# Norm factors of one batch spread by DMA, an FFN group moved, Newton steps one group sooner: attention, RMSnorm and FFN in one kernel

## The chip, the cores and the metric

One core of one Trainium2 chip. The metric is the device time of one execution in microseconds (us). The TensorE clock in the records was 0.998 to 1.0 of full speed, except where it is said otherwise.

## The reference

Eight batches of block-causal attention (8 heads, 576 positions, 64 dimensions a head) feed an RMS norm and a gated FFN (512 to 1536 and back) over all 4608 tokens.

```python
def _attn_ref(q, k, v):                       # q, k, v: 8 x 8 x 576 x 64
    scores = scale * np.matmul(q, k.transpose(0, 1, 3, 2))
    mask = block_i >= block_j                 # blocks of 64 positions
    scores = np.where(mask, scores, -1000000000.0)
    attn = np.exp(scores - max) ; attn = attn / sum     # shortened
    return np.matmul(attn, v)

def _moe_ref(x, w_gate, w_val, w_out, rms_g): # x: 4608 x 512
    rms = np.sqrt(np.mean(x * x, axis=-1, keepdims=True) + 1e-06)
    xn = x / rms * rms_g
    g = xn @ w_gate
    silu = g * (1.0 / (1.0 + np.exp(-g)))
    return silu * (xn @ w_val) @ w_out
```

## The kernel before

TensorE works through one stream in which the attention of one batch is interleaved with FFN work on the batch before. FFN work is dealt out in slots. A call of `group()` fills one slot: either an *up group* (8 matmuls of 512 columns, or 16 of 256 in the first twelve; then tanh on ScalarE and gs and HT on VectorE) or an *output group* (12 matmuls, evacuated by ScalarE alone). There are 108 up groups and 36 output groups in all. `later(k, fn)` runs `fn` k slots later. `mark(n)` says that the tokens below n lie scaled in XT, so that up groups may read them. PSUM is the memory into which matmuls write; its buffers come from two pools, and a matmul must wait until the buffer that it is to write has been read.

```python
    ps_s = ctx.enter_context(tc.tile_pool(name="ps_s", bufs=2, space=PSUM))   # scores, "sps"
    ps_f = ctx.enter_context(tc.tile_pool(name="ps_f", bufs=4, space=PSUM))   # all else, "fps"

    def group(n=1):
        for _ in range(n):
            ...
            if ready and have + 2 <= ui and far >= DOWN0 and (ui == len(ups) or 3 * di <= far - 3):
                ffn_down(*downs[di]); di += 1        # an output group when its turn has come
            elif up:
                ffn_up(*ups[ui]); ui += 1            # else an up group, if its tokens are in XT
            elif ready:
                ffn_down(*downs[di]); di += 1        # else an output group
            clear()
            gone += 1
            ...                                      # run what is due by now

    def ffn_up(n, m, k, lo, w):
        g = ps_f.tile([P, TOKC], FP32, name="fps")
        u = ps_f.tile([P, TOKC], FP32, name="fps")
        ...                                          # 4 matmuls into g, 4 into u
        nc.scalar.activation(out=th, in_=g, func=AF.Tanh, scale=0.5)
        nc.vector.scalar_tensor_tensor(out=gs, in0=th, scalar=1.0, in1=g, op0=ALU.add, op1=ALU.mult)
        nc.vector.tensor_mul(out=HT[n][...], in0=gs..., in1=u...)
```

The norm of a batch goes: sums and squares on TensorE, a transpose and ratios on VectorE, a root step (three small matmuls, then VectorE), two Newton steps of three operations each, and a last product S with a transpose to st. Then the 576 factors of each head must be spread over the partitions. `tail` does that with matmuls against a selection matrix (SELB), `late_tail` by way of DRAM with DMA.

```python
    def norm_spread(key):
        ...
        nc.vector.tensor_mul(out=s32[...], in0=rec[...], in1=y[...])                  # S
        nc.vector.transpose(st[:, 0:32 * n], s32[...])                                # st

    def norm_scale(key, b, j0, width, t):        # spread by matmul, scale from PSUM
        ...
        bc = ps_f.tile([P, 512], FP32, name="fps")
        if t < HP:
            nc.tensor.matmul(bc[:, 0:width], SELB[:, t, :], st[:, 0:width], start=True, stop=True)
            scale(t, j0, width, bc)
        else:
            ...                                  # four matmuls of 64 columns

    def norm_copies(b):                          # spread by DMA
        nc.sync.dma_start(out=rows, in_=nrm[b])                       # st to DRAM
        for a in range(2):
            nc.sync.dma_start(out=bc[a * D:(a + 1) * D], in_=rows....to_broadcast([D, HP, S]))

    def tail(b, k=6):
        norm_sums(b, b, WHOLE); norm_squares(b, b, WHOLE); norm_turn(b)
        if b > 1: norm_ratio(b, True)            # True: w2 summed and split into three bf16 terms
        else:     later(1, norm_ratio, b)
        later(2, norm_root, b)
        later(3, norm_newton, b, 0)
        later(3, norm_newton, b, 1)
        later(4, norm_spread, b)
        for u in range(HP + 1):
            later(k + u // 2, norm_scale, b, b, 0, 512, u)
        ...                                      # marks

    def late_tail(b):
        norm_sums(b, b, WHOLE); norm_squares(b, b, WHOLE); norm_turn(b); norm_ratio(b, True)
        later(2, norm_root, b)
        later(2, norm_newton, b, 0)
        later(3, norm_newton, b, 1)
        later(3, norm_spread, b)
        later(3, norm_copies, b)
        for t in range(HP):
            later(9 + t // 2, norm_apply, b, t)
        later(10, mark, b * S + S)

    for b, t in pairs:                           # batches 2..7, four pairs of heads each
        if (b, t) == (3, 0): ...; later(1, tail, 2, 4)
        e0 = scores_mm(b, t, 0); e1 = scores_mm(b, t, 1)
        scores_exp(*e0)
        group()
        scores_exp(*e1)
        if b > 3 or b == 3 and t == 0:
            group()
        ...
        e2 = scores_mm(b, t, 2)
        last = (b, t - 1) if t else (b - 1, HP - 1)
        outs = values_mm(*last, early=b == 2) if b > 3 or t else []   # early: fps, else sps
        scores_exp(*e2)
        ...
        group()
        evacuate(outs, b == 2)
        if t == 0:
            if b > 3: later(1, late_tail if b > 4 else tail, b - 1)
            scores_ends(b)
        if b > 3 or t == 0: group()
        ...
```

The softmax here doesn't subtract the row's maximum and nothing guards it: scores larger than these inputs give would overflow.

## Time and profile before

| | before |
|---|---|
| time, median of 4 runs | 399.22 us (399.04 to 399.74) |
| span of the profiled execution | 397.72 us |
| VectorE busy | 254.8 us |
| ScalarE busy | 197.3 us |
| moved by DMA | 39.38 MB |

A row of the timeline gives the start, the busy time, the engine, the line, the operation with its tiles and the number of instructions in the row. What stands in brackets is the idle time ahead of it and its releaser. Stalls are measured from start to start throughout, as the prediction explains; most changes between attention matmuls and the rest take 0.09 or 0.10 us more in these traces even where nothing waits, and are called changeovers here. Most rows are shown in the prediction. Two more, of batch 4's norm in the kernel before:

```profile
195.84 1.03 PE L496 MATMUL fps<-XT,WV 128*128 128x512 bf16 x4
196.95 2.75 PE L521 MATMUL fps<-WO,HT 128*128 128x512 bf16 x12
```

The starts are 1.11 apart where 0.866 is the plain pace of four: the stall of 0.25.

### The profile page before, as it was taken

The page shows a single profiled execution, that of the slowest core. Times are in us where ns is not written, and L with a number is a line of the kernel's source. Part 1 is how long each engine was busy: PE and PEld are TensorE (multiplying, and loading weights), DVE is VectorE, ACT ScalarE, POOL GpSimd, SP SyncE. Part 2 cuts the span into 40 slices and gives each one's busy share as a digit, 9 for nine tenths or more (in the row PEclk, how much of TensorE's full clock was granted, in tenths as well). Part 3 has the DMA queues.
Part 4 walks back from the last instruction along what each step waited for, and adds up shares of the span by engine and source line. Part 5 has one row for each costly group of instructions (what it writes and reads, how often), then busy time and mean ns, then how long its engine had stood idle before and what let it go on. Part 6 is the DMA issues. An engine that isn't in the chain of part 4 may idle for free.

```text
span 397.7 us, 7820 instructions
## 1 busy us (share of the span) xinstructions
PE 381.0 (96%) x3064; PEld 180.8 (45%) x3064; DVE 254.8 (64%) x640; ACT 197.3 (50%) x285; POOL 128.3 (32%) x181
## 2 busy tenths in 40 slices
PE   8889899999989999999999999999999899999996
PEld 3457665444434444344444444444344344444443
DVE  4788676567967578657716786478638967654430
ACT  3825871466548655455546564566453233332321
POOL 8927764846039204207446700100020010100000
PEclk9999999999999999999999999999999999999999
DMA  8999999999949919609999995200230020100112
GB/s 110 167 202 190 193 145 153 160 152 163 149 49 135 151 29 92 82 0 120 187 148 153 136 117 114 81 2 1 78 104 2 15 86 28 26 29 26 50 38 98
DMA packets 142677, 39.38 MB, mean 99 GB/s; under 512 B 129457, under 2 KB 139953, under 8 KB 142641
## 3 DMA queue, kind: packets, MB, share of 16 engines
q0 software_dynamic: 108448, 26.75, 69.3%
q1 hardware_dynamic: 33504, 12.00, 19.3%
q8 instruction: 24, 0.39, 0.4%
q10 hardware_dynamic: 688, 0.13, 0.2%
q14 instruction: 13, 0.10, 0.1%
HBM read 41.16 MB, written 10.03 MB: 129 GB/s over the span
## 4 chain that ended last, share of the span: by engine, by line
PE 76%; DVE 11%; DMA 5%; POOL 3%; ACT 2%; issue 1%; DVEq 0%; POOLq 0%
PE fps L496 39%; PE fps L521 23%; PE sps L244 5%; PE sps L293 4%; DMA WG<-in_moe_w_gate_dram 3%; DVE HT L504 3%; DVE gs L502 2%; PE fps L333 2%; DMA nt<-in_q_dram 2%; PE fps L293 1%; POOL VB L126 1%; POOL nt L112 1%; DVE st L426 1%; ACT PT L253 1%; ACT th L500 1%
## 5 line engine op out<-in xcount | busy, mean ns | idle before, releaser
L496 PE MATMUL fps<-XT,WG 128*128 128x512 bf16 (+1 forms) x480 | 112.1, 359 | 3.9 <-DVE gs L502 1.9
L502 DVE SCALAR_TENSOR_TENSOR gs<-th,fps 128x512 bf16<-128x512 f32 x108 | 73.9, 684 | 58.4 <-ACT th L500 58.2
L496 PE MATMUL fps<-XT,WV 128*128 128x512 bf16 (+1 forms) x480 | 111.0, 358 | 0.0
L253 ACT ACTIVATE PT<-sps 128x1024 bf16<-128x1024 f32 (+1 forms) x96 | 93.2, 988 | 30.7 <-PE sps L244 30.3
L500 ACT ACTIVATE th<-fps 128x512 f32<-128x512 f32 x108 | 64.6, 598 | 77.1 <-PE fps L496 74.1
L521 PE MATMUL fps<-WO,HT 128*128 128x512 bf16 (+1 forms) x444 | 97.1, 373 | 0.1
L504 DVE TENSOR_TENSOR HT<-gs,fps 128x512 bf16<-128x512 bf16 x108 | 74.3, 688 | 12.3 <-PE fps L496 0.9
L496 PEld LDWEIGHTS <-WV 128*128 128x128 bf16 x480 | 46.9, 98 | 47.1 <-issue 1.0
L496 PEld LDWEIGHTS <-WG 128*128 128x128 bf16 x480 | 42.4, 97 | 52.4 <-issue 17.2
L521 PEld LDWEIGHTS <-HT 128*128 128x128 bf16 x444 | 42.6, 98 | 50.5 <-issue 3.0
L525 POOL DMA_DIRECT2D out_dram<-osb x22 | 12.6, 571 | 153.2 <-ACT osb L523 151.3
L523 ACT ACTIVATE osb<-fps 128x512 f32<-128x512 f32 (+1 forms) x37 | 21.7, 586 | 78.7 <-PE fps L521 68.6
L126 POOL DMA_DIRECT2D VB<-in_v_dram x48 | 39.5, 847 | 6.0 <-DMA nt<-in_q_dram 2.7
L244 PE MATMUL sps<-QT,KT 64*128 64x192 bf16 (+5 forms) x280 | 32.3, 308 | 3.1 <-DVE KT L209 1.0
L119 POOL DMA_DIRECT2D nt<-in_q_dram x30 | 26.3, 876 | 7.0 <-DMA VB<-in_v_dram 4.0
L119 POOL DMA_DIRECT2D nt<-in_k_dram x30 | 26.3, 877 | 6.5 <-DMA VB<-in_v_dram 2.9
L319 DVE TENSOR_TENSOR SQ<-OT 128x512 bf16<-128x512 bf16 (+1 forms) x44 | 15.9, 372 | 10.2 <-ACT OT L317 9.3
L293 PEld LDWEIGHTS <-VB 128*64 128x64 bf16 x344 | 14.5, 109 | 13.1 <-issue 5.2
L441 DVE SCALAR_TENSOR_TENSOR XT<-OT,gscale,fps 128x64 bf16<-128x64 bf16 (+5 forms) x36 | 15.0, 477 | 8.0 <-PE fps L448 8.0
L244 PEld LDWEIGHTS <-KT 64*128 64x128 bf16 x280 | 8.8, 94 | 24.8 <-issue 19.6
L529 POOL DMA_DIRECT2D out_dram<-osb x12 | 6.5, 544 | 41.3 <-ACT osb L523 41.3
L226 DVE MEMSET PT<- 64x64 uint32 x95 | 8.9, 112 | 14.3 <-ACT PT L253 11.1
(77 smaller groups left out, 227.7 us busy)
## 6 DMA issues: line engine op xcount, KB each, us to landing
out_dram<-osb POOLq DMA_DIRECT2D x22, 256.0 KB, 2.4
VB<-in_v_dram POOLq DMA_DIRECT2D x32, 128.0 KB, 6.1
nt<-in_q_dram POOLq DMA_DIRECT2D x24, 128.0 KB, 6.7
nt<-in_k_dram POOLq DMA_DIRECT2D x24, 128.0 KB, 7.3
bc<-rows SPq DMA_DIRECT2D x8, 288.0 KB, 4.7
WG<-in_moe_w_gate_dram POOLq DMA_DIRECT2D x4, 384.0 KB, 9.6
WV<-in_moe_w_val_dram POOLq DMA_DIRECT2D x4, 384.0 KB, 10.8
WO<-in_moe_w_out_dram POOLq DMA_DIRECT2D x4, 384.0 KB, 7.8
```

The source lines that it names most:

```text
L119: nc.gpsimd.dma_start(out=nt[0:rows, 0:512].rearrange("p (h d) -> p h d", h=H), in_=src[b, :, c * P:c * P + rows, :].rearrange("h p d -> p ...
L126: nc.gpsimd.dma_start(out=vb[r:r + n, cc, :].rearrange("p (h d) -> p h d", h=H), in_=v[b, :, tok:tok + n, :].rearrange("h p d -> p h d"))
L244: nc.tensor.matmul(sp[:, a, o:o + w], KT[b][r, t, c * P:(c + 1) * P], QT[b][r, t, q0:q0 + w], start=True, stop=True, skip_group_check=True)
L253: nc.scalar.activation(out=pt[:, :, lo:lo + width], in_=sp[:, :, 0:width], func=AF.Exp, scale=SCALE)
L293: nc.tensor.matmul(ov[a * D:(a + 1) * D, o:o + w], vb[:, c, h * D:(h + 1) * D], rhs, start=(i == 0), stop=(i == len(chunks) - 1), skip_gro ...
L319: nc.vector.tensor_mul(out=sq, in0=o, in1=o)
L496: nc.tensor.matmul(acc[:, i * w:(i + 1) * w], wt[c][:, p, r * P:(r + 1) * P], XT[:, p, x0:x0 + w], start=(p == 0), stop=(p == HP - 1), ski ...
L500: nc.scalar.activation(out=th, in_=g, func=AF.Tanh, scale=0.5)
L502: nc.vector.scalar_tensor_tensor(out=gs, in0=th, scalar=1.0, in1=g, op0=ALU.add, op1=ALU.mult)
L504: nc.vector.tensor_mul(out=HT[n][:, m:m + k, lo:lo + w], in0=gs.rearrange("p (k w) -> p k w", k=k), in1=u.rearrange("p (k w) -> p k w", k=k))
L521: nc.tensor.matmul(po[:, 0:step], HT[n][:, m, i * P:(i + 1) * P], WO[:, m, o:o + step], start=(m == 0), stop=(m == NMC - 1))
L523: nc.scalar.mul(out=osb[:, o:o + step], in_=po[:, 0:step], mul=0.5)
```

## The change

The intent: let the norm factors of batch 3 go by DMA as those of later batches already do, take the Newton steps of batches 1 and 2 a slot sooner so that TensorE waits less for st, and put one FFN group fewer ahead of the last score step of batch 4's first pair.

```diff
@@ tail
         later(2, norm_root, b)
-        later(3, norm_newton, b, 0)
-        later(3, norm_newton, b, 1)
-        later(4, norm_spread, b)
+        later(2, norm_newton, b, 0)
+        later(2, norm_newton, b, 1)
+        later(3, norm_spread, b)
@@ loop over the pairs
-        if b > 3 or b == 3 and t == 0:
+        if b > 3 and (b, t) != (4, 0) or (b, t) == (3, 0):
             group()
@@
-                later(1, late_tail if b > 4 else tail, b - 1)
+                later(1, late_tail, b - 1)
```

## The prediction

> **What bounds the kernel now.** I read the page first (busy shares and the chain that ended last), then the timeline around the norm of batch 2, of batch 3, and of the later batches whose norm factors already go by DMA.
>
> ```profile
> span 397.7 us, 7820 instructions
> ...
> PE 381.0 (96%) x3064; PEld 180.8 (45%) x3064; DVE 254.8 (64%) x640; ACT 197.3 (50%) x285; POOL 128.3 (32%) x181
> ...
> PE 76%; DVE 11%; DMA 5%; POOL 3%; ACT 2%; issue 1%; DVEq 0%; POOLq 0%
> ```
>
> TensorE is busy 381.0 of 397.7 us at full clock, so what can be won is matmuls taken away, or gaps in its stream closed. A busy share cannot show a short gap, because overlapping matmul records hide it; I therefore take starts. In the chain of waits twelve output matmuls of 512 columns take 2.59 us, 0.216 each; a row of four takes 0.866. A start that comes later than that is a stall. Counted so, the stalls over 0.1 us after the first 60 us make about 9 us. One of the largest is ahead of the scaling of batch 2:
>
> ```profile
> 110.71 0.17 DVE L403 TENSOR_SCALAR y<-sh 128x18 int32<-128x18 int32 x1
> ...
> 110.73 2.76 PE L521 MATMUL fps<-WO,HT 128*128 128x512 bf16 x12
> 110.80 0.68 DVE L502 SCALAR_TENSOR_TENSOR gs<-th,fps 128x512 bf16<-128x512 f32 x1
> 111.58 0.69 DVE L504 TENSOR_TENSOR HT<-gs,fps 128x512 bf16<-128x512 bf16 x1
> 112.18 0.17 DVE L410 SCALAR_TENSOR_TENSOR z<-y 128x18 f32<-128x18 f32 x1
> ...
> 113.45 0.20 DVE L423 TENSOR_TENSOR S<-rec,y 128x36 bf16<-128x36 f32 x1
> ...
> 113.69 0.78 DVE L426 STREAM_TRANSPOSE st<-S 128x576 bf16<-128x576 bf16 x1
> ...
> 114.52 0.59 PE L448 MATMUL fps<-st,SELB 128*128 128x512 bf16 x2 [1.02 <-DVE st L426]
> ```
>
> The output group started at 110.73 and should have made room at 113.32; the spreading matmuls start at 114.52, 1.2 us late, released by st. This is the wait that the Newton part aims at. What the reader is to see is that VectorE has no hole between 110.71 and 114.47: gs, HT, six Newton steps at 0.21 us each, S, st, one behind the other.
>
> Batch 3 pays for its spread on TensorE and once more behind it:
>
> ```profile
> 156.89 0.59 PE L448 MATMUL fps<-st,SELB 128*128 128x512 bf16 x2
> ...
> 157.41 0.39 PE L244 MATMUL sps<-QT,KT 64*128 64x320 bf16 x4
> ...
> 161.11 0.59 PE L448 MATMUL fps<-st,SELB 128*128 128x512 bf16 x2
> ...
> 161.55 0.59 PE L496 MATMUL fps<-XT,WG 128*128 128x512 bf16 x2
> ...
> 162.33 0.38 PE L496 MATMUL fps<-XT,WG 128*128 128x512 bf16 x1 [0.19 <-DVE XT L441]
> ...
> 162.99 0.38 PE L496 MATMUL fps<-XT,WG 128*128 128x512 bf16 x1 [0.28 <-DVE XT L441]
> ...
> 164.07 0.28 PE L452 MATMUL fps<-st,SELB 128*128 128x64 bf16 x4
> ...
> 164.28 0.58 PE L244 MATMUL sps<-QT,KT 64*128 64x512 bf16 x4
> ```
>
> The spreading matmuls hold the stream for 0.52 + 0.44 + 0.21 = 1.17 us (start to the next start). The first FFN group on the new tokens then waits twice for XT: 162.33 instead of 161.98, and 162.99 instead of 162.55, 0.79 us in all.
>
> The later batches show what a DMA spread costs instead:
>
> ```profile
> 237.59 1.03 PE L496 MATMUL fps<-XT,WV 128*128 128x512 bf16 x4
> 239.01 1.02 PE L496 MATMUL fps<-XT,WG 128*128 128x512 bf16 x4 [0.40 <-DVE gs L502]
> ```
>
> For batch 5 the stream should go on at 238.45 and does so at 239.01, 0.56 us late: Newton, S, st and a square sit ahead of gs on VectorE, and gs gives back the PSUM buffer that the next group needs. By the same subtraction batch 6 loses 0.92 (at 280.56), batch 4 only 0.25 (at 196.95); batch 4 has an output group, which needs VectorE for nothing, among its FFN groups there.
>
> **What the Trainium skill says.** "Perfetto Trace Analysis", Identifying the Most-Contended Engine: matmul busy time is no good measure of headroom, since pipelined records mislead. The trace agrees: 96% busy, and a stall of 1.2 us is listed as 1.02. "TensorE: Matmul & The Clock Gate", Back-to-back issue gap: about 216 ns for 512 columns for isolated matmuls, but about 131 ns sustained in a stream with weight loads. This trace has weight loads ahead of all of them and shows 216; I use that. "VectorE: DVE Perf Modes", The DRAIN you can't avoid: an operation does not start until the one before has drained, so operation count is what to save. The Newton steps, 18 elements each, stand 0.21 us apart here: moving them saves none. "DMA: Bandwidth & Descriptors", Two DMAs through the same engine are not ordered: a DMA that reads what another wrote must wait for its completion. Here bc is issued 4.6 us after rows for batch 4 (196.03 to 200.66) and 1.8 us for batch 6.
>
> **The change part by part.**
>
> Newton sooner. This touches batches 1 and 2 only. In batch 1 the instruction order of VectorE comes out the same. In batch 2 the six Newton steps now precede gs and HT of the last FFN group before the output group; spread comes before the output group's slot instead of after. But output groups put nothing on VectorE, so the same instructions stand ahead of st as before, with no hole among them, and st still ends at about 114.5. The six steps (6 x 0.21 = 1.3 us) now delay gs and HT: HT ends at about 113.55 instead of 112.27, and the twelfth output matmul, which reads it and was due at 113.11, waits some 0.45 us. That comes out of the 1.2 us that TensorE waits anyway. Gain 0.0; perhaps 0.1 lost through the score exponential behind the later output evacuation.
>
> Batch 3 by DMA. Eight matmuls go with their loads: -1.17 us. The scaling on VectorE becomes four operations of 0.81 us from SBUF, issued while output groups run, nine and ten group slots after the sums: the waits for XT go, -0.79 us. New: rows and two bc transfers on SyncE, and a possible wait of gs behind st as in the other batches. An output group comes directly after the root step, so Newton, S and st fall in its 2.6 us: I take 0.05 us.
>
> One group less ahead of batch 4's last score step. The group is moved, not removed: 108 up and 36 output groups stay. What changes is the time that ScalarE has for the exponentials. With a single group there, batch 3 shows this wait:
>
> ```profile
> 128.00 0.39 PE L244 MATMUL sps<-QT,KT 64*128 64x320 bf16 x4
> ...
> 128.70 0.22 PE L293 MATMUL sps<-P,VB 128*64 128x64 bf16 x2 [0.30 <-ACT PT L253]
> ```
>
> The scores take 0.33 us, so the value matmuls are 0.37 late. For batch 4: the second exponential ran 133.54 to 134.45 before; the scores would now start at 133.71 and the values be due at 134.04, so about 0.4 us is new.
>
> Everything later comes one group sooner. In batch 4's norm no output group falls among the FFN groups any more (the last four of that stretch come in a row earlier). It then looks like batches 5 and 6: (0.56 + 0.92) / 2 = 0.74 instead of 0.25, +0.49 us.
>
> Sum: -1.17 - 0.79 + 0.05 + 0.40 + 0.49 + 0.0 to 0.1, about -1.0 us. **399.26 - 1.0 = 398.3 us.**
>
> **The rivals.** First, the Newton step removes the 1.2 us: then 397.1. For it: the releaser named is st, and Newton is in its chain. Against: the VectorE queue without a hole. It would need gs or HT to stand behind st instead of ahead. Second, bc is late for batch 3. For batch 4 VectorE waited for it, and the group that reads XT comes soon after:
>
> ```profile
> 208.56 1.55 DVE L477 SCALAR_TENSOR_TENSOR XT<-OT,gscale,bc 128x576 bf16<-128x576 bf16 x2 [3.50 <-DMA bc<-rows]
> ...
> 212.92 1.04 PE L496 MATMUL fps<-XT,WG 128*128 128x512 bf16 x4
> ```
>
> The last scaling ended at 212.54, 0.4 us ahead. Batch 3 has the same four output groups and value matmuls ahead of its reader, and around 140 to 157 the DMA engines have less to do (65 GB/s against 162 in 180 to 197); two microseconds later than there would cost one or two: 399.5 to 400.5. Third, the shifted groups clump VectorE work elsewhere: worth 0.5 us each way at most, by the stalls that batches 5 to 7 show. Fourth, the move is free (no wait on the exponential, batch 4's stall unchanged): then -1.9, 397.4.
>
> **Range and chances.** The removed 1.96 us are the surest part; the three additions (0.9 together) may lie between 0.2 and 1.7. Runs before spread over 0.7 us. So 397.3 to 399.4. Two per cent are 8 us, more than all the stalls concerned together: faster 0.01, within 0.985, slower 0.005.
>
> **What would show it.** Right: the matmul count falls by 8; st of batch 2 still ends 3.7 to 3.9 us after y of the root step, and the wait ahead of its spreading matmuls plus one inside the output group before it still sums to about 1.2; no wait for XT at the first group of batch 3's tokens; value matmuls in batch 4's first pair waiting 0.3 to 0.5 on ScalarE; a wait on gs of over 0.4 us in batch 4's norm. Wrong: st of batch 2 a microsecond earlier; bc of batch 3 landing after the output groups; a new wait over 0.5 us on a transpose or on K or Q.

## The result and the profile after

| | before | after |
|---|---|---|
| median | 399.22 us (4 runs) | 398.01 us (397.46 to 398.09, 4 runs) |
| span of the profiled execution | 397.72 | 396.24 |
| VectorE busy | 254.8 | 254.6 |
| ScalarE busy | 197.3 | 197.3 |
| moved by DMA | 39.38 MB | 40.11 MB |

The ratio is 0.9965 (95% interval 0.9947 to 0.9982). A ratio is the mean time of one kernel's fast runs over that of the other's of the same rounds, so it is not quite the ratio of the medians quoted. 398.3 had been predicted, with a range of 397.3 to 399.4. All outputs are right.

The page of the kernel after, in its first lines and the shares of the chain that ended last:

```profile
span 396.2 us, 7766 instructions
...
PE 376.6 (95%) x3016; PEld 180.1 (45%) x3056; DVE 254.6 (64%) x636; ACT 197.3 (50%) x285; POOL 128.4 (32%) x181
...
PE 77%; DVE 9%; DMA 5%; POOL 4%; ACT 3%; issue 2%; DVEq 0%; POOLq 0%
```

The weight loads tell the true count: 3056 instead of 3064, eight fewer. The matmul records are 48 fewer, because 40 of them are missing from this trace. So the fall of PE's busy time from 381.0 to 376.6 is no measure of the gain. The VectorE share of the chain fell from 11% to 9%.

The timeline of the kernel after, around batch 2's norm:

```profile
113.62 0.39 PE L521 MATMUL fps<-WO,HT 128*128 128x512 bf16 x1 [0.33 <-DVE HT L504]
113.71 0.78 DVE L426 STREAM_TRANSPOSE st<-S 128x576 bf16<-128x576 bf16 x1
114.54 0.59 PE L448 MATMUL fps<-st,SELB 128*128 128x512 bf16 x2 [0.53 <-DVE st L426]
```

st starts at 113.71 where it started at 113.69, and the spreading matmuls at 114.54 where they started at 114.52. The single wait of 1.20 us has become two: 0.49 ahead of the last output matmul, which now waits for a later HT, and 0.70 ahead of the spread, 1.19 together.

Batch 3's scaling on VectorE, in the kernel after:

```profile
161.21 1.55 DVE L477 SCALAR_TENSOR_TENSOR XT<-OT,gscale,bc 128x576 bf16<-128x576 bf16 x2 [0.87 <-DMA bc<-rows]
...
166.26 1.55 DVE L477 SCALAR_TENSOR_TENSOR XT<-OT,gscale,bc 128x576 bf16<-128x576 bf16 x2
```

and the first group that reads those tokens, on TensorE:

```profile
168.19 1.04 PE L496 MATMUL fps<-XT,WG 128*128 128x512 bf16 x4
```

VectorE waited 0.87 us for bc, with nothing else to do. The last scaling ended at 166.26 + 1.55 = 167.81, 0.4 us ahead of its reader, as batch 4's did before. There is no wait for XT any more.

Batch 4's first pair, and batch 4's norm sixty microseconds later, both in the kernel after:

```profile
133.95 0.39 PE L244 MATMUL sps<-QT,KT 64*128 64x320 bf16 x4
...
134.65 0.22 PE L293 MATMUL sps<-P,VB 128*64 128x64 bf16 x2 [0.30 <-ACT PT L253]
```

```profile
192.86 1.03 PE L496 MATMUL fps<-XT,WV 128*128 128x512 bf16 x4
194.29 1.02 PE L496 MATMUL fps<-XT,WG 128*128 128x512 bf16 x4 [0.41 <-DVE gs L502]
```

The values start 0.70 after the scores instead of 0.33 (135.53 to 135.86 in the kernel before): 0.37 lost there. Measured as a stall it is 0.46, but 0.09 of that is the changeover, which the kernel before has too. In the norm the next group starts 1.43 after the last instead of 0.866: a stall of 0.57, where it was 0.25.

The two traces, stage by stage, against the terms of the prediction (us; the sizes are starts against starts):

| term | predicted | measured |
|---|---|---|
| batch 3's spread and its waits for XT | -1.17 - 0.79 + 0.05 = -1.91 | -1.77 |
| Newton sooner, batch 2 | 0.0 to +0.1 | +0.14 |
| value matmuls wait for an exponential | +0.40 | +0.38 |
| batch 4's wait for gs | +0.49 | +0.32 |
| batch 6's wait for gs, 0.92 to 0.57 | not foreseen | -0.35 |
| last matmul to the end of the span, 4.09 to 3.89 | not foreseen | -0.20 |
| sum | about -1.0 | -1.48 (span: -1.48; medians: -1.21) |

For the first row: from batch 3's sums to batch 4's sums it took 42.41 us before and 41.50 after. The stretch after holds one up group less (8 x 0.216 = 1.73) and one output group more (2.59), so 0.86 us more work: -0.91 - 0.86 = -1.77. No wait for gs is seen in batch 3's norm. The third row is from the start of batch 4's first scores to batch 3's sums (9.36 us before, 8.01 after with one up group less, 1.73).

### The profile page after: what moved, and what is told of

Its sections match the earlier page's. It is cut to its first block, busy times and chain, and to the rows that moved or that the text cites. A ratio compares the mean times of both kernels' runs of the same rounds, so it can differ in the third digit from the quotient of the medians.

```text
span 396.2 us, 7766 instructions
## 1 busy us (share of the span) xinstructions
PE 376.6 (95%) x3016; PEld 180.1 (45%) x3056; DVE 254.6 (64%) x636; ACT 197.3 (50%) x285; POOL 128.4 (32%) x181
## 2 busy tenths in 40 slices
DMA packets 143364, 40.11 MB, mean 101 GB/s; under 512 B 129504, under 2 KB 140640, under 8 KB 143328
## 4 chain that ended last, share of the span: by engine, by line
PE 77%; DVE 9%; DMA 5%; POOL 4%; ACT 3%; issue 2%; DVEq 0%; POOLq 0%
PE fps L496 40%; PE fps L521 23%; PE sps L244 5%; PE sps L293 4%; DMA WG<-in_moe_w_gate_dram 3%; DVE HT L504 2%; PE fps L333 2%; DMA nt<-in_q_dram 2%; DVE gs L502 2%; PE fps L293 1%; ACT PT L253 1%; POOL VB L126 1%; POOL nt L112 1%; DVE st L426 1%; ACT th L500 1%
## 5 line engine op out<-in xcount | busy, mean ns | idle before, releaser
L496 PE MATMUL fps<-XT,WG 128*128 128x512 bf16 (+1 forms) x460 | 110.3, 358 | 4.7 <-DVE gs L502 1.9
L477 DVE SCALAR_TENSOR_TENSOR XT<-OT,gscale,bc 128x576 bf16<-128x576 bf16 (+2 forms) x24 | 15.9, 714 | 1.1 <-DMA bc<-rows 0.9
```

The costliest lines, as they stand in the source:

```text
L496: nc.tensor.matmul(acc[:, i * w:(i + 1) * w], wt[c][:, p, r * P:(r + 1) * P], XT[:, p, x0:x0 + w], start=(p == 0), stop=(p == HP - 1), ski ...
```

## The experiments

Eight kernels on one chip shared the runs of the kernel before: 399.40 us (399.32 to 399.77, 9 runs). The last two ran later on another chip.

### Newton steps alone

The kernel before with the first hunk of the change only.

```diff
-        later(3, norm_newton, b, 0)
-        later(3, norm_newton, b, 1)
-        later(4, norm_spread, b)
+        later(2, norm_newton, b, 0)
+        later(2, norm_newton, b, 1)
+        later(3, norm_spread, b)
```

> The kernel before with the Newton part alone (Newton two group slots and spread three slots after the sums of the first norms). My theory: VectorE's queue has no hole between the root step and st of batch 2, so st ends at the same time (y of the root step to the start of st: 2.98 us, as before), the 1.2 us wait only splits in two (about 0.5 inside the output group, 0.7 ahead of the spreading matmuls), and the time changes by 0.0 to +0.15 us. Rival: the wait was for Newton, st comes about 1 us sooner and the time falls by 1.0 to 1.2 us.

Measured: 399.41 us (399.20 to 400.04), ratio 1.0 (0.9987 to 1.0014). TensorE in its timeline:

```profile
113.50 0.39 PE L521 MATMUL fps<-WO,HT 128*128 128x512 bf16 x1 [0.33 <-DVE HT L504]
...
114.42 0.59 PE L448 MATMUL fps<-st,SELB 128*128 128x512 bf16 x2 [0.53 <-DVE st L426]
```

The same two waits, 0.49 and 0.70, with nothing else changed. The rival that sooner Newton steps remove the 1.2 us is out.

### DMA for batch 3 alone

The kernel before with the third hunk only.

```diff
-                later(1, late_tail if b > 4 else tail, b - 1)
+                later(1, late_tail, b - 1)
```

> The kernel before with only batch 3's factors spread by DMA; the group ahead of batch 4's scores stays. My theory: -1.17 us for eight matmuls and -0.79 for the waits for XT; +0.25 for a wait on gs in batch 3's norm (an output group stands ahead of its root step, as in batch 4 before); +0.32 because batch 4's norm loses its output group already by this part (0.57 instead of 0.25). Sum -1.4 us, which would be more than the whole change gave in the traces when their noise is taken off (-1.0). Rival, as the prediction put it: the wait in batch 4's norm comes from dropping the group, then -1.7 here and 0.25 us kept in batch 4's norm.

Measured: 397.68 us (397.05 to 398.03), ratio 0.9954 (0.9941 to 0.9966): -1.7 where -1.4 had been expected. TensorE in batch 4's norm:

```profile
195.13 1.03 PE L496 MATMUL fps<-XT,WV 128*128 128x512 bf16 x4
...
196.55 1.02 PE L496 MATMUL fps<-XT,WG 128*128 128x512 bf16 x4 [0.40 <-DVE gs L502]
```

1.42 between the starts: the wait for gs is 0.56 here already, without the moved group. Batch 3's own norm has a wait of 0.25 at 154.50. Batch 6's wait is 0.56 instead of 0.92, which is about the 0.35 us by which this run was better than expected. By its time alone the run would fit the rival as well, which said -1.7 with the 0.25 of batch 4 kept; the 0.56 in the trace is what rules that out.

### The moved group alone

The kernel before with the second hunk only.

```diff
-        if b > 3 or b == 3 and t == 0:
+        if b > 3 and (b, t) != (4, 0) or (b, t) == (3, 0):
```

> The kernel before with only the group ahead of batch 4's last score step dropped. My theory: +0.46 us by the value matmuls of batch 4's first pair that wait for the exponential; the waits for XT at batch 3's first group stay (0.79 us); batch 4's wait on gs goes from 0.25 to under 0.1, since an output group then follows its root step. Sum +0.2 us, between 0.0 and +0.5. Rival (the prediction's): batch 4's wait grows to 0.57, then +0.8 us.

Measured: 399.32 us (398.97 to 399.56), ratio 0.9995 (0.9982 to 1.0007). TensorE in batch 4's first pair:

```profile
134.09 0.22 PE L293 MATMUL sps<-P,VB 128*64 128x64 bf16 x2 [0.31 <-ACT PT L253]
```

and in batch 4's norm:

```profile
194.07 1.03 PE L496 MATMUL fps<-XT,WV 128*128 128x512 bf16 x4
194.94 1.03 PE L496 MATMUL fps<-XT,WG 128*128 128x512 bf16 x4
```

The wait of the values is there, 0.47 with the changeover. Batch 4's wait for gs is not: 0.87 between the starts is the plain pace, so even the 0.25 of before is gone. So the group's move costs 0.38, gives 0.25 back, and leaves +0.13. The trace shows +0.14, when the 0.44 us by which this execution was already ahead at 30 us are taken out. The medians show -0.08 where +0.2 had been expected: the spread of the runs does not resolve so little, and the sign rests on the trace alone. The kernel after, however, has 0.57 in batch 4's norm. With the run before, this puts that wait to the DMA part. The way there is read from the code and the traces: the tokens of batch 3 are marked ready later, output groups bridge the time in a row (five with the DMA part alone, from 154.50 on, four in the kernel after, two in the kernel before), and none is left to fall among batch 4's norm.

### The change without its Newton part

The kernel after with the first hunk undone; it serves as the base of the next experiments.

> The changed kernel with the Newton steps and the spread of the first norms put back to three and four slots. My theory: it is as fast as the changed kernel or 0.15 us faster; the wait ahead of batch 2's spreading matmuls is 1.2 us in one piece again, and the step of 0.14 us that the changed kernel loses at the value matmuls after it goes away. Rival: 1.0 to 1.2 us slower than the changed kernel.

Measured: 397.81 us (397.31 to 398.85; the slowest at a clock of 0.996), ratio 0.996 (0.9947 to 0.9972). The wait of 1.19 ahead of the spread is in one piece again. Span 396.13 against 396.24: the Newton part gains nothing, and costs 0.1 us if anything.

### Fewer VectorE operations ahead of st

The last kernel, with batch 2's ratio not split into three bf16 terms: six small operations fewer in the VectorE queue, and two fp32 terms instead of three bf16 ones in the matmuls of the root step.

```diff
-        if b > 1:
-            norm_ratio(b, True)
+        if b == 2:
+            norm_ratio(b)
         else:
             later(1, norm_ratio, b)
```

> The changed kernel with the old Newton places, and batch 2's norm ratio without its split in three bf16 terms: six small VectorE operations (6 x 0.21 = 1.28 us) fewer ahead of st, two fp32 terms in the root step instead. If the wait ahead of batch 2's spreading matmuls is set by the length of a VectorE queue without holes, st ends some 1.2 us sooner against the root step's neighbours and the 1.2 us wait goes to under 0.1; fp32 matmuls in the root step cost some 0.3 to 0.4 (0.52 busy for four in batch 1's root step against 0.22 for three bf16). Net against the kernel with the old Newton places: -0.7 to -0.9 us. If st waits for something else than its queue, it does not move and the time rises by 0.3.

Measured: 397.06 us (396.77 to 397.24), ratio 0.9937 (0.9923 to 0.995), so -0.75 against the base and -0.66 in the span. VectorE in its timeline:

```profile
112.73 0.78 DVE L426 STREAM_TRANSPOSE st<-S 128x576 bf16<-128x576 bf16 x1
```

and TensorE:

```profile
113.56 0.59 PE L448 MATMUL fps<-st,SELB 128*128 128x512 bf16 x2 [0.32 <-DVE st L426]
...
114.73 0.22 PE L293 MATMUL sps<-P,VB 128*64 128x64 bf16 x2 [0.25 <-ACT PT L253]
```

st starts at 112.73, 1.0 us earlier than the 113.74 of the base. The wait for it is 0.49 instead of 1.19, because the output group ahead of it comes earlier too (110.48 instead of 110.79: a wait of 0.49 for HT at 108.42 in the base is gone as well). Of the 1.0 us not all arrives: the scores now come closer behind the exponential, and the values behind them wait 0.41 on ScalarE. The expectation that under 0.1 of the wait would be left was a miss for that reason; the net was met. The place of the Newton steps is worth nothing and the number of operations is worth nearly a microsecond: what is ahead of st in the queue is the cause.

### The other Newton order in the later batches

The kernel after, with the second Newton step of `late_tail` a slot sooner, ahead of a gs and an HT.

```diff
         later(2, norm_newton, b, 0)
-        later(3, norm_newton, b, 1)
+        later(2, norm_newton, b, 1)
```

> The changed kernel with the second Newton step of the later batches (3 to 7) in the group of the root step, so 0.64 us less VectorE work stands between that group's gs and the next one's. A reader of the waits alone would expect the wait on gs in batches 4 to 6 (0.57 each) to vanish, -1.7 us or more. My theory: VectorE has no hole from the root step to that gs either, the work ahead of it is the same, and the wait stays at 0.57: 0.0 us, within 0.2.

Measured: 397.66 us (397.27 to 398.17), ratio 0.9955 (0.9942 to 0.9967), span 396.38. TensorE in batch 5's norm:

```profile
235.62 1.02 PE L496 MATMUL fps<-XT,WG 128*128 128x512 bf16 x4 [0.40 <-DVE gs L502]
```

The waits of batches 4, 5 and 6 are 0.57, 0.56 and 0.56, as in the kernel after (0.57 each). Batch 7's 0.88 came out as 0.32 + 0.57. The same rule, shown in other places: an instruction moved within a queue without a hole changes nothing for what stands behind both places.

### An output group behind the root step

The change without its Newton part, with an output group put by force right behind the root step of batches 4 to 7.

```diff
-            if ready and have + 2 <= ui and far >= DOWN0 and (...):
+            if ready and gone in (56, 72, 88, 102) or ready and have + 2 <= ui and far >= DOWN0 and (...):
```

> The changed kernel with the old Newton places, and one output group (no VectorE work) put directly after the root step of batches 4 to 7 in place of later. If the wait on gs in these norms comes from VectorE falling behind in an unbroken row of FFN groups, it goes: -0.57 for each of batches 4, 5, 6 and -0.88 for the one behind batch 7's st; the 1.0 us around batch 7's root step stays. Sum -2.6 us against the kernel with the old Newton places, so about 395.2 us. If the prediction's cause (the group count ahead of the scores) is what matters, nothing changes.

Measured: 396.29 us (396.23 to 396.58), ratio 0.9921 (0.9908 to 0.9935). All waits for gs in the four norms are gone, 2.58 us. But only 1.5 us of them arrive: 395.2 had been expected, a miss. TensorE at the first group on batch 7's tokens:

```profile
320.64 0.38 PE L496 MATMUL fps<-XT,WG 128*128 128x512 bf16 x1 [0.35 <-DVE XT L477]
321.37 0.38 PE L496 MATMUL fps<-XT,WG 128*128 128x512 bf16 x1 [0.35 <-DVE XT L477]
```

With the output group spent earlier, this group follows directly behind the scaling of its tokens and waits twice, 0.51 + 0.52 = 1.03. That the waits vanish as foretold fits their cause: too much VectorE work per TensorE work in that stretch. An output group, which brings VectorE nothing, lets it catch up. What TensorE waits for there is a PSUM buffer that gs gives back; whether more buffers would do as well was not tried.

### Batch 3's values in another PSUM pool

The change without its Newton part, with the value matmuls of batch 3 written to the pool of four banks (fps) instead of that of the scores (sps).

```diff
-        outs = values_mm(*last, early=b == 2) if b > 3 or t else []
+        apart = b < 4 or (b, t) == (4, 0)
+        outs = values_mm(*last, early=apart) if b > 3 or t else []
+        if (b, t) == (4, 0):
+            outs.append(head_product(3, ps_f.tile([P, 512], FP32, name="fps")))
```

> The changed kernel with the old Newton places, and the values of batch 3 accumulated in a bank of the other PSUM pool, so that they don't wait for the second exponential to free its bank. If that bank is what the value matmuls wait for, the waits of 0.35, 0.47 and 0.47 us at batch 3's pairs and batch 4's first go (-1.3 us) and possibly the 0.58 and 0.15 ahead of the scores behind them (up to -2.3); the dropped group then costs nothing. If they wait for the exponential's own data, nothing goes.

Measured: 395.94 us (395.71 to 396.36), ratio 0.9912 (0.9899 to 0.9926). ScalarE and TensorE in batch 4's first pair:

```profile
131.92 0.91 ACT L253 ACTIVATE PT<-sps 128x896 bf16<-128x896 f32 x1
132.18 0.39 PE L244 MATMUL sps<-QT,KT 64*128 64x320 bf16 x4
132.50 0.22 PE L293 MATMUL fps<-P,VB 128*64 128x64 bf16 x2
```

0.32 between scores and values where the kernel after has 0.70; the exponential still runs, until 132.83, when the values start. All the waits of this kind in batch 3 (0.35, 0.47, 0.47) and those ahead of the score matmuls there (0.58, and some of 0.10 to 0.15) are down to the changeover, and the time is 1.9 us below that of the base. The spans differ by 1.94, of which 0.34 had already come by 101 us, ahead of the edit's first effect, so some 1.6 us are the edit's by the traces. So the term "+0.40" of the prediction is not a wait for the result of an exponential. The value matmuls, which are those of the pair before, do not need it: they wait until ScalarE has read the bank (the PSUM buffer) that they are to write.

### The change again, and all that helped together

On another chip, the change unchanged, and a kernel with the last three edits (operations, output group, pool), no Newton part, and batch 7's tokens marked ready a slot later, against the wait that the output group had brought.

```diff
-        later(10, mark, b * S + S)
+        later(11 if b == B - 1 else 10, mark, b * S + S)
```

> The changed kernel once more, unchanged, in five rounds, so that it can be set beside the single parts, which had five rounds each. By the sum of the traces it should lie 0.2 to 0.4 us above the kernel with only the DMA part (397.68) and 0.1 to 0.2 above the one without the Newton part (397.81): 397.9 to 398.1. If the parts were worth what the change's order suggests, it would be the fastest of the three.

> All that the runs found to pay, together: DMA spread for batch 3, the dropped group, old Newton places, the values of batch 3 in the other PSUM pool (-1.9 by its run), an output group after each root step (-2.6), the ready mark of batch 7 one slot later so that the group reading XT does not come right behind its scaling (the new wait of 1.0 us in the run with the output groups), and batch 2's ratio without its split (-0.75). If these waits are independent, 397.81 - 1.9 - 2.6 - 0.75 = 392.6 us, all waits on gs in the norms gone; if they hide behind one another, between that and 394.5.

Measured, the change again: 397.73 us (397.26 to 398.14, 6 runs), below the 397.9 to 398.1 expected. Against 397.68 of the DMA part alone and 397.81 without the Newton part, the three can't be told apart by time; only the spans of the traces (396.24 and 396.34 for the change, 395.90 and 396.13 for the others) put them in the order that was expected. The kernel before had 401.01 us here (398.83 to 401.76, 11 runs), six of its runs at a clock of 0.991 to 0.996, so the recorded ratios of this call to it (0.9929 for the change; 0.9797, 0.9769 to 0.9825, for all together, verdict "unclear") are not leaned on.

All together: 392.36 us (391.95 to 392.78, 5 runs), 0.9865 of the change on the same chip, where 392.6 had been expected. Against the five runs of the kernel before at full clock (398.83 to 399.81 on this chip) it is some 1.7% faster by the means (392.4 over 399.3), an estimate from few runs. Its busy times:

```profile
PE 378.4 (97%) x3057; PEld 179.9 (46%) x3057; DVE 255.7 (65%) x630; ACT 196.9 (50%) x285; POOL 128.6 (33%) x181
```

No wait for gs in a norm is left; what is left are single stalls of 0.3 to 0.7 us.

## Why the prediction was right, point by point

**Newton sooner: right.** The wait split into 0.49 + 0.70, where 0.45 of the 1.2 had been predicted for the first; the part alone took 399.41 against 399.40. The loss of "perhaps 0.1" was 0.14 in the trace, at the place named: the values at 115.51 start 0.44 after their scores instead of 0.32. The reason given, a queue without a hole, is shown from two sides: the order of the Newton steps changes nothing in batch 2 nor in batches 4 to 7, and six operations fewer bring st 1.0 us forward.

**Batch 3 by DMA: right.** -1.77 instead of -1.91. The term -1.17 was mis-sized: counted to the next start it holds 0.10 of changeover twice, which the stream has without these matmuls too. The matmuls themselves take 4 x 0.216 + 4 x 0.029 = 0.98, and -0.98 - 0.79 is the measured -1.77. The term taken as +0.05, a wait for gs of its own, is nothing in the kernel after, and 0.25 in the DMA part alone. The last scaling was in time by the predicted 0.4 us, so the second rival is out.

**The moved group: right in size, its cause left open.** 0.38 instead of 0.40. The prediction reckoned with the end of the second exponential and did not say why the values have to wait for it. The other pool shows that it is not for the result: the values wait for ScalarE to free the scores' bank.

**Batch 4's wait for gs: right in direction by luck, with a wrong cause.** +0.32 was measured; +0.49 was predicted, because the mean of batches 5 and 6 (0.74) was taken where 0.57 came out. That mean held batch 6's 0.92, of which 0.36 were a pause of another kind (next point). And "everything later comes one group sooner" is not what made it: the moved group alone removes this wait, the DMA part alone makes it 0.56. That no output group falls among that norm any more was right.

**What was not foreseen.** -0.35 in batch 6. In the kernel before, VectorE paused there between gs and HT for no reason that the trace shows:

```profile
271.62 0.68 DVE L502 SCALAR_TENSOR_TENSOR gs<-th,fps 128x512 bf16<-128x512 f32 x1
...
272.76 0.69 DVE L504 TENSOR_TENSOR HT<-gs,fps 128x512 bf16<-128x512 bf16 x1 [0.46 <-PE fps L496]
```

The releaser named is a matmul whose stream had run on unhindered. Such a pause comes at up to three fixed places in the VectorE queue (instructions 284, 502 and 603 of 640 in the kernel before and in the one with the Newton part alone), at one in the DMA part alone, at two in the moved group alone, and in none of the kernel after, the one without the Newton part and the four built for single causes. Counted with VectorE's semaphore instructions in the packed traces, the HT that follows each of the nine pauses is the 320th, 576th or 704th instruction, a multiple of 64. Of the 1296 HTs in the twelve traces 11 stand at such a multiple, and no other has the pause; the two without it, both 640th, show that the place alone does not decide. So a few instructions fewer ahead of it, whatever they did, can move the pause away: this part of the gain is luck. Where the one in the middle vanishes, batch 6's wait goes from 0.92 to 0.56. That it is the cause of the difference is read from the traces and no experiment was built for it; what makes the pause stays open. The same holds for the 0.2 us at the end of the span, seen in every kernel with batch 3 by DMA.

The terms that were foreseen sum to -0.93 in the traces, against about -1.0. The two unforeseen ones made it -1.48; in the medians it is -1.21.

## What to carry to other kernels

A stall's releaser is not its cause: count what stands ahead of it in its engine's queue. If that queue has no hole, moving an instruction forward in it gains nothing; take operations out, or let work pass that this engine has no part in. When work changes its pace, ask where the groups that used to fill other gaps have gone: data marked ready later drew the output groups together here, and the stall came up a batch later. And a short wait of matmuls on another engine may be for the bank, not for the data: another PSUM pool for batch 3's values was worth more than the whole change (397.81 to 395.94, so 1.9 us, against 1.2; 1.6 against 1.5 by the traces).

## What the Trainium skill lacked or had wrong

- "TensorE: Matmul & The Clock Gate", Back-to-back issue gap: the sustained figure of about 131 ns for 512 columns in a stream of load and matmul pairs is not seen here. Twelve such matmuls, each with its weight load ahead, take 2.59 us, 216 ns each, which is what the page gives for an isolated matmul, and in its section on the clock for back-to-back ones.
- "Perfetto Trace Analysis", Optimization Strategy: it advises to make the dependencies of a gap start sooner or complete faster. It lacks that "sooner" inside a full in-order queue gains nothing: 1.0 (0.9987 to 1.0014) for batch 2's Newton steps, and waits of 0.56 to 0.57 us unchanged in batches 4 to 6; six operations fewer gave 0.75 us. What it says there on consistent bubbles, that too little PSUM can be the reason, agrees: 0.35 to 0.47 us for the values of three pairs of batch 3, gone with another pool.
- No page has the pause of 0.46 us of VectorE between two dependent operations, seen nine times, each time at a multiple of 64 in its instructions; its cause is open.
